# A row-form tail, and sixteen rows of one load moved to three DMA engines, in a four-layer decode attention kernel

## Chip, cores, metric

One core of one Trainium2 chip. The metric is the device time of one execution in microseconds (us), as the median of several runs; less is better.

## The reference

Four attention layers with one query token each, A, B, A, B, each with its residual. The two caches of a layer are 32 heads x 8192 positions x 192 in bfloat16; A and B have their own, and both are read twice.

```python
def _A_ref(x, k_cache, v_cache, wq, wo):          # _B_ref is the same with B's inputs
    q = (x @ wq).reshape(B, Sq, Hq, Dh) ...        # B = Sq = 1, D = 640, 32 heads of 192
    scores = einsum("bhqd,bhkd->bhqk", q, k) * (Dh ** -0.5)
    p = softmax(scores, axis=-1)
    o = einsum("bhqk,bhkd->bhqd", p, v)
    return o ... .reshape(B, Sq, Hq * Dh) @ wo
x = A_x
x = x + _A_ref(_layernorm(x), ...)                 # layer 0
x = x + _B_ref(_layernorm(x), ...)                 # layer 1
x = x + _A_ref(_layernorm(x), ...)                 # layer 2
return x + _B_ref(_layernorm(x), ...)              # layer 3
```

## The kernel before

The kernel walks 16 pairs of heads per layer. K and V of a pair are laid over 128 partitions, and `pool` is a ring of eight slots of `TS` = 12,288 columns (24,576 B in each partition) into which all loads go, in one queue issued by SyncE. `op` adds an instruction to an engine's list, with the events that it waits for; `need` issues loads up to the one asked for.

"V15" is V of a layer's last pair. In the B layers (1 and 3) its first half is one ordinary load of 128 rows of 24,576 B, and its second half comes as two quarters, the last with its own semaphore, so that the products of the last pair can start early:

```python
def transfer(n):
    ...
    if n[0] in "kv":
        h = 2 * pair(l, n[2])
        r = w[n[0]][0, h:h + 2].rearrange("h (p j) d -> (h p) (j d)", j=J)
        if quarters(n):                            # second half of V15 in layers 1 and 3
            x = TS // 2
            if n in landed:
                return SP.op(lambda s: s.dma_start(t[:, x:], r[:, TS + x:]), sem=semVQ, inc=16)
            return SP.op(lambda s: s.dma_start(t[:, 0:x], r[:, TS:TS + x]), *free, sem=semS[i], inc=16)
        if whole(*n[:3]):
            ...
        else:
            f = lambda s: s.dma_start(t, r[:, n[3] * TS:(n[3] + 1) * TS])   # V15's first half
    ...
    return SP.op(f, *free, sem=semS[i], inc=16)
```

The output projection makes y as a column, five columns of 128, with 128 columns of weights for each one-column matmul:

```python
def project(n, w, o, ev_o):
    t3 = w.rearrange("p (i n) -> p i n", n=D)
    k = t3.shape[1]
    PE.wait(ev_o, need(n), last["YB"])
    for i in range(k):
        for c in range(DC):                        # DC = 5
            e = PE.op(lambda t, i=i, c=c, ...: t.matmul(
                YB[:, c:c + 1], lhsT=t3[:, i, c:D:DC], rhs=o[:, i:i + 1], ...), ...)
    ...
```

In layer 3 the last steps are the last quarter of V15, its products, the projections of the last rows, x + y, and the result:

```python
if p == NPAIR - 1 and i == rounds // 4 and quarters(("v", nl, np_, u)):
    PE.wait(need(("vq", l)))                       # the last quarter of V15
...
if l + 1 == NL:
    return None, DV.op(lambda v: v.tensor_tensor(x_bf[:], x_true[:], YB[:, 0:DC], ALU.add), ev_y, ev_true, bank=YBu)
...
e = SP.op(lambda s: s.dma_start(out[0, 0].rearrange("(p c) -> p c", c=DC), x_bf[:]), ev_true, sem=semOUT, inc=16)
```

Of the kernel before, what the change touches and what calls it, by code (L numbers as in the profile page):

```python
# [5 lines left out]
ALU = mybir.AluOpType  # L6
# [62 lines left out]
def build(nc, A_x, A_k, A_v, A_wq, A_wo, B_x, B_k, B_v, B_wq, B_wo, out):  # L69
# [28 lines left out]
    with ExitStack() as ctx:  # L98
        def sb(name, shape, dt):
            return ctx.enter_context(nc.sbuf_tensor(name, shape, dt))  # L100
# [43 lines left out]
        vs = col(1)  # L144
        rs = col(1)
        xb = sb("xb", [P, DC], BF16)

        QM = ps("QM")
        SP_ = [ps("S0"), ps("S1")]
        OY = ps("OY", 4)  # L150
        O = OY[:, 0:VK * DH]
        YB = OY[:, VK * DH:]
        TB = ps("TB")
        use = {b: {} for b in ("QM", "S0", "S1", "O", "TB", "YB")}
        QMu, Ou, TBu, YBu = [(use[b],) for b in ("QM", "O", "TB", "YB")]
# [17 lines left out]
                                        base=0, pattern=[[-1, P]], channel_multiplier=1), e)  # L173
        PO.op(lambda g: g.memset(ones[:], 1.0))
        PO.op(lambda g: g.memset(one_b[:], 1.0))
        mask = acc[:, 0:2 * VK].rearrange("p (h i) -> p h i", h=2)
        e = PO.op(lambda g: g.memset(mask, 0.0))
        for t in range(G):
# [159 lines left out]
        def transfer(n):  # L338
            l = n[1]
            o = ORDER[l]  # L340
            w = W[l % 2]
            free = [freed[b] for b in before[n]]
            if n[0] == "wol":
                r0 = o["wol"] * PD
                return SP.op(lambda s: s.dma_start(
                    rows[:], w["wo"][r0:r0 + PD].rearrange("(p i) n -> p (i n)", p=P)),
                    *free, sem=semOL, inc=16)
            if n[0] == "t":
                return max(free, key=lambda e: e[1]) if free else None
            if n[0] == "wob":  # L350
                r0 = o["wo"][2] * PD
                return SP.op(lambda s: s.dma_start(
                    slot[place[("wo", l, 2)]][:, (NW - NB[l]) * D:NW * D],
                    w["wo"][r0:r0 + PAIRS_W * PD].rearrange("(p i) n -> p (i n)", p=P)[:, (NW - NB[l]) * D:]),
                    sem=semOB, inc=16)
            if n[0] == "vq":
                n = ("v", l, NPAIR - 1, 1)
            i = place[n]
            t = slot[i]
# [3 lines that stand above are left out]
                if quarters(n):  # L363
                    x = TS // 2
                    if n in landed:
                        return SP.op(lambda s: s.dma_start(t[:, x:], r[:, TS + x:]), sem=semVQ, inc=16)
                    return SP.op(lambda s: s.dma_start(t[:, 0:x], r[:, TS:TS + x]), *free, sem=semS[i], inc=16)
                if whole(*n[:3]):
                    if n[3] == 1:
                        return landed[n[:3] + (0,)]  # L370
                    f = lambda s: s.dma_start(pool[:, i * TS:(i + 2) * TS], r)
                else:
                    f = lambda s: s.dma_start(t, r[:, n[3] * TS:(n[3] + 1) * TS])
            elif n[0] == "wq" and l < 2:
                f = lambda s: s.dma_start(pool[:, i * TS:i * TS + DC * QW], w["wq"].rearrange("(p c) n -> p (c n)", c=DC))
            elif n[0] == "wq":
                c0, k = Q_PARTS[n[2]]
                f = lambda s: s.dma_start(
                    wq_rows(l, n[2]),
                    w["wq"][:, o["q1"] * PD:o["q1"] * PD + QC].rearrange("(p c) n -> p c n", c=DC)[:, c0:c0 + k, :])  # L380
            else:
                r0 = o["wo"][n[2]] * PD
                k = NW - NB[l] if n[2] == 2 else NW
                f = lambda s: s.dma_start(
                    t[:, 0:k * D], w["wo"][r0:r0 + PAIRS_W * PD].rearrange("(p i) n -> p (i n)", p=P)[:, 0:k * D])
            return SP.op(f, *free, sem=semS[i], inc=16)
# [53 lines left out]
        def layer(l, ev_z, ev_true):  # L440
# [82 lines left out]
            def project(n, w, o, ev_o):  # L523
# [11 lines left out]
                    freed[n] = e  # L535
                return e

            def columns(k):

                PE.wait(last["row_written"], last["TT"], ev_const)  # L540
                for i in range(k):
                    e = PE.op(lambda t, i=i: t.matmul(TB[:, i:i + 1], lhsT=orow[:, i:k * P:k], rhs=one_b[96:97, :],
                                                      start=True, stop=True), signal=(i == k - 1), bank=TBu)
                last["orow"] = freed[n] = e
                last["TT"] = AC.op(lambda a: a.activation(oT[:, 0:k], TB[:, 0:k], ACT.Copy),  # L545
                                   e, last["oT"], bank=TBu)
# [55 lines left out]
            def values(p, us=(0, 1)):  # L602
# [19 lines left out]
                for r in range(us[0] * rounds // 2, (us[-1] + 1) * rounds // 2):  # L622
                    u, i = divmod(r, rounds // 2)
                    u = turn[nl, np_][u]
                    PE.wait(need(("v", nl, np_, u)))
                    t = slot[place[("v", nl, np_, u)]]
                    if p == NPAIR - 1 and i == rounds // 4 and quarters(("v", nl, np_, u)):
                        PE.wait(need(("vq", l)))
                    for c in range(k * DH // N):
                        for g in range(G):  # L630
                            j = (i * G + g) * k
                            o, x, y = (O[32 * g:32 * g + 2 * k, c * N:(c + 1) * N],
                                       p_sb[par][:, u * JU + j:u * JU + j + k, :].rearrange("p j h -> p (j h)"),
                                       t[:, j * DH + c * N:j * DH + (c + 1) * N])
                            f, fin = r == 0, r == rounds - 1
                            e = PE.op(lambda t, c=c, g=g, o=o, x=x, y=y, f=f, fin=fin: (
                                t.matmul(o, lhsT=x, rhs=y, start=f, stop=fin) if c == 0 else  # L637
                                matmul_held(t, o, x, y, f, fin, 32, 32 * g)),
                                signal=(fin and c == k * DH // N - 1 and g == G - 1), bank=Ou)
# [43 lines left out]
            for n in [n for n in steps if n[1] == l]:  # L683
                if n[0] == "m":
                    products(*n[2:])
                elif n[0] == "s":
                    softmax(n[2])
                elif n[0] == "v":
                    values(n[2], n[3:] or (0, 1))
                elif n[0] == "e":  # L690
                    gather(n[2])
                elif n[0] == "busy":
                    busy(n[2])
                elif n[0] == "wqr":
                    q_rows(n[2], 1)
                elif n[0] == "wq":
                    q_rows(n[2], 0, 1 if l == 2 and n[2] == 0 else None)
                    q_ready = n[2] == 2 or q_ready
                elif n[0] == "wc":
                    columns(NW)  # L700
                    last["oTw"] = last["TT"]
                elif n[0] == "wo":
                    k = NW - NB[l] if n[2] == 2 else NW
                    last["oT"] = project(n, slot[place[n]][:, 0:k * D], oT[:, 0:k], last["oTw"])
                elif n[0] == "wob":
                    last["oT"] = freed[("wo", l, 2)] = project(
                        n, slot[place[("wo", l, 2)]][:, (NW - NB[l]) * D:NW * D], oT[:, NW - NB[l]:NW], last["oTw"])
                else:
                    last["TT"] = last["TTn"]
                    last["oTl"] = ev_y = project(n, rows[:], oTl, last["TTn"])  # L710
                    if l == 1:
                        busy(2)
                if q_ready and (n[0] == "wq" and l >= 2 or n[0] == "m" and n[3] == 1):
                    following = n[2] + 1 if n[0] == "m" else 1
                    if following < NPAIR and following not in ev_q:
                        q_spread(following)
                ahead()
            if l + 1 == NL:
                return None, DV.op(lambda v: v.tensor_tensor(x_bf[:], x_true[:], YB[:, 0:DC], ALU.add), ev_y, ev_true, bank=YBu)
            ev_z = DV.op(lambda v: v.tensor_tensor(z[:], xc[:], YB[:, 0:DC], ALU.add), ev_y, ev_xc, bank=YBu)  # L720
            e = DV.op(lambda v: v.tensor_tensor(x_true[:], x_true[:], YB[:, 0:DC], ALU.add), ev_y, ev_true, bank=YBu)
            last["YB"] = e
# [1 line left out]

        for l in range(NL):
            ev_z, ev_true = layer(l, ev_z, ev_true)
        e = SP.op(lambda s: s.dma_start(out[0, 0].rearrange("(p c) -> p c", c=DC), x_bf[:]), ev_true, sem=semOUT, inc=16)
        SP.wait(e)
        assert issued[0] == len(plan)

# [51 lines left out]
```

## Time and profile before

| | kernel before |
|---|---|
| median time | 1984.8 us (1984.23 to 1985.38) |
| profiled run | span 1983.6 us |
| busy: PE, DVE | 64%, 61% |
| load queue | 848.38 MB, 99.5% of the time of 16 DMA engines |
| stream, about 430 GB/s, ends at | 1978.1 us |
| last quarter of V15 landed, from there to the end | 1975.1, 8.5 us |

The kernel is bound by its loads: 848 MB at 428 GB/s. The lines that carry this stand in the prediction. One more view is used later: the stretches around the end of layer 1, in the kernel before. The columns are the stretch, its length, the busy time of PE, PEld, DVE, ACT and POOL, then the granted clock, the DMA share (1.00 is sixteen busy engines) and GB/s.

```profile
960.00:988.00 28.00, 20.72 (x83) 0.60 (x8) 25.36 (x19) 1.56 (x6) 0.00 (x0) 0.86 0.99 426
988.00:1012.00 24.00, 20.21 (x224) 5.87 (x159) 9.56 (x18) 1.89 (x7) 0.00 (x0) 0.86 0.96 395
1012.00:1040.00 28.00, 23.89 (x196) 4.91 (x94) 16.48 (x22) 3.85 (x8) 0.55 (x1) 0.87 1.00 417
```

In the middle stretch the rate dips a little, where the small last loads of the layer are.

### The profile page before, as it was taken

Reading aid. Unit: us, or ns where it says so; the run is one execution under the profiler, and the core shown is the slowest. Engines: PE = TensorE matmul, PEld = TensorE weight load, DVE = VectorE, ACT = ScalarE, POOL = GpSimd, SP = SyncE. Lnnn points to the kernel's source line nnn. Section 1 sums busy time; section 2 is a strip of 40 time slices with the busy share of each in tenths; the row PEclk is TensorE's granted clock in tenths of the full one; section 3 lists DMA queues with packets and bytes.
Section 4 is the critical chain, followed back from the end, with each engine's and each line's share of the span. In section 5 each row is a group of like instructions: output and inputs, shape, how many; then the busy total and the mean of one; then the engine's idle time right before and its main releaser. Section 6 shows DMA issues by size and latency. Waiting matters only on the chain.

```text
span 1983.6 us, 13955 instructions
## 1 busy us (share of the span) xinstructions
PE 1276.7 (64%) x8352; PEld 149.3 (8%) x3271; DVE 1200.5 (61%) x1371; ACT 139.5 (7%) x461; POOL 4.4 (0%) x22
## 2 busy tenths in 40 slices
PE   3567477666466665666785675665676765665657
PEld 0001001000100100100020010010002001001001
DVE  3566467467166656656745565665664774665665
ACT  0000000000000000000010000000000000000000
POOL 0000000000000000000000000000000000000000
PEclk9787777778687777787887777878886887778779
DMA  9999999999999999999999999999999999999998
GB/s 412 440 430 430 430 438 430 429 433 430 432 434 435 429 429 435 431 432 430 429 408 434 425 428 435 428 430 429 431 431 428 435 427 436 430 434 433 431 430 345
DMA packets 26926, 849.25 MB, mean 428 GB/s; under 512 B 3184, under 2 KB 3184, under 8 KB 3952
## 3 DMA queue, kind: packets, MB, share of 16 engines
q1 hardware_dynamic: 26720, 848.38, 99.5%
q8 instruction: 45, 0.74, 0.2%
q14 instruction: 17, 0.14, 0.0%
q10 hardware_dynamic: 144, 0.00, 0.0%
HBM read 848.36 MB, written 0.00 MB: 428 GB/s over the span
## 4 chain that ended last, share of the span: by engine, by line
DMA 67%; DVE 16%; PE 16%; ACT 1%; issue 0%; SPq 0%
DMA pool<-in_B_k_cache_dram 27%; DMA pool<-in_A_v_cache_dram 20%; DMA pool<-in_A_k_cache_dram 14%; DVE pool L560 14%; PE S L58 7%; DMA pool<-in_B_v_cache_dram 6%; PE OY L58 5%; PE OY L637 3%; DVE acc L656 1%; ACT p_sb L597 1%; DVE s_sb L582 1%; PE S L573 0%; PE OY L530 0%; DVE m_bf L584 0%; PE QM L587 0%
## 5 line engine op out<-in xcount | busy, mean ns | idle before, releaser
L560 DVE TENSOR_TENSOR pool<-pool,q_sb 128x3072 bf16<-128x3072 bf16 x512 | 861.1, 1754 | 241.0 <-DMA pool<-in_B_k_cache_dram 142.8
L58 PE MATMUL S<-pool,ident 128*128 128x512 bf16 x2944 | 784.6, 422 | 23.1 <-DVE pool L560 22.1
L667 PE MATMUL TB<-acc,small 128*1 128x192 f32 x240 | 80.6, 485 | 212.0 <-DVE acc L656 212.0
L573 PE MATMUL S<-pool,ident 128*128 128x512 bf16 x128 | 62.2, 486 | 213.9 <-DVE pool L560 213.9
L58 PE MATMUL OY<-pool,p_sb 128*16 128x512 bf16 x1920 | 199.7, 491 | 0.0
L655 DVE TENSOR_SCALAR acc<-OY,small 128x192 f32<-128x192 f32 x64 | 26.8, 418 | 278.0 <-PE OY L58 247.8
L637 PE MATMUL OY<-pool,p_sb 128*16 128x512 bf16 (+1 forms) x1216 | 147.0, 492 | 64.2 <-DMA pool<-in_A_v_cache_dram 57.8
L656 DVE SCALAR_TENSOR_TENSOR acc<-OY,small,acc 128x192 f32<-128x192 f32 x424 | 177.1, 418 | 14.9
L582 DVE TENSOR_REDUCE s_sb<-S 128x64 f32<-128x512 f32 x128 | 88.3, 690 | 68.6 <-PE S L58 68.6
L519 ACT ACTIVATE q_sb<-QM 128x192 bf16<-128x192 f32 x60 | 19.9, 331 | 954.7 <-PE QM L513 954.7
L678 ACT ACTIVATE rows<-TB,small 1x192 bf16<-1x192 f32 x120 | 43.2, 405 | 585.8 <-PE TB L667 585.8
L651 DVE RECIPROCAL small<-TB 1x2 f32<-1x2 f32 x64 | 11.2, 175 | 94.3 <-PE TB L612 75.3
L597 ACT ACTIVATE p_sb<-s_sb,small 64x128 bf16<-64x128 f32 x128 | 55.7, 435 | 162.2 <-DVE small L591 161.4
L573 PEld LDWEIGHTS S<-pool,ident 128*128 128x128 bf16 x128 | 12.9, 101 | 684.7 <-DVE pool L560 659.9
L612 PE MATMUL TB<-small,ones 128*1 128x2 f32 x120 | 11.4, 165 | 74.0 <-ACT p_sb L597 74.0
L637 PEld LDWEIGHTS OY<-pool,p_sb 128*16 128x16 bf16 (+1 forms) x1216 | 39.1, 106 | 206.2 <-issue 133.7
L587 PE MATMUL QM<-ident,m_bf 128*64 128x64 bf16 x128 | 14.0, 216 | 54.4 <-DVE m_bf L584 53.9
L667 PEld LDWEIGHTS TB<-acc,small 128*1 128x1 f32 x240 | 19.6, 100 | 311.0 <-DVE acc L656 284.7
L530 PE MATMUL OY<-oT,pool 128*128 128x1 bf16 x900 | 38.2, 178 | 2.8 <-ACT oT L545 2.8
L530 PEld LDWEIGHTS OY<-oT,pool 128*128 128x128 bf16 x900 | 37.1, 131 | 4.9 <-ACT oT L545 3.6
L591 DVE TENSOR_REDUCE small<-QM 128x1 f32<-128x64 f32 x64 | 14.4, 224 | 35.4 <-PE QM L587 35.4
L513 PEld LDWEIGHTS QM<-rows,one_b 1*64 1x64 bf16 x120 | 6.2, 100 | 349.4 <-issue 343.5
(62 smaller groups left out, 195.3 us busy)
## 6 DMA issues: line engine op xcount, KB each, us to landing
pool<-in_B_k_cache_dram SPq DMA_DIRECT2D x28, 6144.0 KB, 38.2
pool<-in_B_v_cache_dram SPq DMA_DIRECT2D x28, 6144.0 KB, 33.3
pool<-in_A_v_cache_dram SPq DMA_DIRECT2D x27, 6144.0 KB, 27.6
pool<-in_A_k_cache_dram SPq DMA_DIRECT2D x34, 3072.0 KB, 20.2
pool<-in_A_k_cache_dram SPq DMA_DIRECT2D x14, 6144.0 KB, 36.2
pool<-in_A_v_cache_dram SPq DMA_DIRECT2D x10, 3072.0 KB, 14.7
pool<-in_B_k_cache_dram SPq DMA_DIRECT2D x8, 3072.0 KB, 23.0
pool<-in_A_wo_dram SPq DMA_DIRECT2D x6, 2400.0 KB, 22.0
```

The costliest lines, as they stand in the source:

```text
L58: return t.add_instruction(mybir.InstMatmult(name=t.bass.get_next_instruction_name(), engine=mybir.EngineType.PE, ins=[t.lower_ap(rhs), t. ...
L519: lambda a: a.activation(q_sb[i][:], QM[:, 0:DH], ACT.Copy), e, last["q"][i], bank=QMu)
L530: e = PE.op(lambda t, i=i, c=c, f=y_first[0], fin=n[0] == "wol" and i == k - 1: t.matmul(YB[:, c:c + 1], lhsT=t3[:, i, c:D:DC], rhs=o[:, i ...
L560: e = DV.op(lambda v, d0=d0: v.tensor_tensor(k3[:, :, d0:d0 + QD], kin[:, :, d0:d0 + QD], q_sb[qi][:, d0:d0 + QD].unsqueeze(1).broadcast_t ...
L573: t.matmul(S[:, :], lhsT=ident[:], rhs=k3[:, :, d0:d0 + R], start=True, stop=fin) if d0 == 0 else
L582: lambda v, u=u: v.tensor_reduce(s[:, u * JU:(u + 1) * JU], SP_[u][:].rearrange("p (j r) -> p j r", r=R), AX.X, ALU.add), ev_S[p, u], last ...
L597: ev_p[p] = AC.op(lambda a, h=h, r=r: a.activation(p_sb[par][r, :, h], s[r, :], ACT.Exp, bias=negm[par][r, 0:1], accum_out=l_col[par][r, h ...
L637: t.matmul(o, lhsT=x, rhs=y, start=f, stop=fin) if c == 0 else
L655: v.tensor_scalar(acc[:], O[:, 0:DH], pick[:, 0:1], None, ALU.mult) if i == 0 else
L656: v.scalar_tensor_tensor(out=acc[:], in0=O[:, i * DH:(i + 1) * DH], scalar=pick[:, i:i + 1], in1=acc[:], op0=ALU.mult, op1=ALU.add)), e if ...
L667: e = PE.op(lambda t, h=h: t.matmul(TB[96:97, C_O + h * DH:C_O + (h + 1) * DH], lhsT=half[:, h:h + 1], rhs=acc[:], start=True, stop=True), ...
L678: last["TO"] = last["row_written"] = AC.op(lambda a, h=h: a.activation(orow[:, o0 + h * DH:o0 + (h + 1) * DH], TB[96:97, C_O + h * DH:C_O ...
```

## The change

Two ideas. The first is to take load off most DMA engines: of V15's first half, 112 rows go as one transfer, and 16 rows as five transfers of three rows and one of one row, meant for three DMA engines that the author took to be among those that end early. The prediction calls them 0, 1 and 2; these are names. The second is a shorter tail: the last projections and the result as a row (two halves of 320), x + y turned into that row beforehand, six matmuls that are only to keep the clock up before the last wait, and a result that leaves as two runs of 640 B.

```diff
+                if n[0] == "v" and n[2:] == (NPAIR - 1, 0) and l % 2:
+                    ends = [0] + list(range(112, P, 3)) + [P]
+                    for x, y in zip(ends, ends[1:]):
+                        e = SP.op(lambda s, x=x, y=y: s.dma_start(t[x:y, :], r[x:y, 0:TS]), *free, sem=semS[i], inc=16)
+                    return e
...
+            def to_row(ev):                        # after layer 3's second output projection
+                e = DV.op(lambda v: v.tensor_tensor(z[:], x_true[:], YB[:, 0:DC], ALU.add), ev, ev_true, bank=YBu)
+                ... three bfloat16 parts of z: 3 copies, 2 subtractions on DVE
+                ... 1 matmul to zero YR, 30 small ones to place the parts as a row
+            def project_row(n, w, o, ev_o):
+                ...
+                for i in range(k):
+                    for h in range(2):
+                        e = PE.op(lambda t, ...: t.matmul(
+                            YR[32 * h:32 * h + 1, :], lhsT=o[:, i:i + 1], rhs=t3[:, i, h * HD:(h + 1) * HD], ...), ...)
...
+                        if l == 3:
+                            busy(6)
                         PE.wait(need(("vq", l)))
...
-                    last["oTl"] = ev_y = project(n, rows[:], oTl, last["TTn"])
+                    last["oTl"] = ev_y = (project_row if l == 3 else project)(n, rows[:], oTl, last["TTn"])
... (likewise for layer 3's other last projections)
-                return None, DV.op(lambda v: v.tensor_tensor(x_bf[:], x_true[:], YB[:, 0:DC], ALU.add), ev_y, ev_true, bank=YBu)
+                a, m = slot[place[("wo", 3, 2)]][0:33, 0:HD], 192
+                return a, (DV.op(lambda v: v.tensor_copy(a[:, 0:m], YR[:, 0:m]), ev_y, last["oT"], bank=YBu),
+                           AC.op(lambda c: c.activation(a[:, m:], YR[:, m:], ACT.Copy), ev_y, last["oT"], bank=YBu))
...
-        e = SP.op(lambda s: s.dma_start(out[0, 0].rearrange("(p c) -> p c", c=DC), x_bf[:]), ev_true, sem=semOUT, inc=16)
+        e = SP.op(lambda s: s.dma_start(out[0, 0].rearrange("(h n) -> h n", h=2), ev_z[0:33:32, :]), *ev_true, sem=semOUT, inc=16)
```

More of the change, by code (lines that the diff above doesn't have):

```diff
@@ L146, in build @@
         xb = sb("xb", [P, DC], BF16)
+        zero = sb("zero", [P, 33], BF16)
+        part = [sb(f"part{i}", [P, DC], BF16) for i in range(3)]
         QM = ps("QM")
@@ L152, in build @@
         YB = OY[:, VK * DH:]
+        HD = D // 2
+        YR = YB[0:33, 64:64 + HD]
         TB = ps("TB")
@@ L175, in build @@
         PO.op(lambda g: g.memset(one_b[:], 1.0))
+        PO.op(lambda g: g.memset(zero[:], 0.0))
         mask = acc[:, 0:2 * VK].rearrange("p (h i) -> p h i", h=2)
@@ L536, in project @@
                 return e
+            def to_row(ev):
+                src = z
+                e = DV.op(lambda v: v.tensor_tensor(z[:], x_true[:], YB[:, 0:DC], ALU.add), ev, ev_true, bank=YBu)
+                for i in range(3):
+                    e = DV.op(lambda v, i=i: v.tensor_copy(part[i][:], z[:]), e)
+                    if i < 2:
+                        e = DV.op(lambda v, i=i: v.tensor_tensor(z[:], z[:], part[i][:], ALU.subtract), e)
+                PE.wait(e, ev_const)
+                PE.op(lambda t: t.matmul(YR, lhsT=zero[:], rhs=ident[:, 0:1].broadcast_to([P, HD]), start=True, stop=False,
+                                         skip_group_check=True), signal=False, bank=YBu)
+                for i in range(3):
+                    for c in range(DC):
+                        for h in range(2):
+                            e = PE.op(lambda t, i=i, c=c, h=h: t.matmul(
+                                YR[32 * h:32 * h + 1, c:HD:DC], lhsT=part[i][:, c:c + 1], rhs=ident[:, 64 * h:64 * h + 64],
+                                start=False, stop=False, skip_group_check=True), signal=(i == 2 and c == DC - 1 and h == 1), bank=YBu)
+            def project_row(n, w, o, ev_o):
+                t3 = w.rearrange("p (i n) -> p i n", n=D)
+                k = t3.shape[1]
+                PE.wait(ev_o, need(n))
+                for i in range(k):
+                    for h in range(2):
+                        e = PE.op(lambda t, i=i, h=h, fin=n[0] == "wol" and i == k - 1: t.matmul(
+                            YR[32 * h:32 * h + 1, :], lhsT=o[:, i:i + 1], rhs=t3[:, i, h * HD:(h + 1) * HD], start=False, stop=fin,
+                            skip_group_check=True), signal=(i == k - 1 and h == 1), bank=YBu)
+                return e
             def columns(k):
@@ L703, in layer @@
                     k = NW - NB[l] if n[2] == 2 else NW
-                    last["oT"] = project(n, slot[place[n]][:, 0:k * D], oT[:, 0:k], last["oTw"])
+                    last["oT"] = (project_row if l == 3 and n[2] == 2 else project)(n, slot[place[n]][:, 0:k * D], oT[:, 0:k], last["oTw"])
+                    if l == 3 and n[2] == 1:
+                        to_row(last["oT"])
                 elif n[0] == "wob":
-                    last["oT"] = freed[("wo", l, 2)] = project(
+                    last["oT"] = freed[("wo", l, 2)] = (project_row if l == 3 else project)(
                         n, slot[place[("wo", l, 2)]][:, (NW - NB[l]) * D:NW * D], oT[:, NW - NB[l]:NW], last["oTw"])
```

## The prediction

> **What bounds the kernel now.** I read the page first, then the stretches of the last layer, the timeline of the last 30 us, the end of the second layer, and last the completion records of the transfers.
>
> ```profile
> PE 1276.7 (64%) x8352; PEld 149.3 (8%) x3271; DVE 1200.5 (61%) x1371; ACT 139.5 (7%) x461; POOL 4.4 (0%) x22
> q1 hardware_dynamic: 26720, 848.38, 99.5%
> DMA 67%; DVE 16%; PE 16%; ACT 1%; issue 0%; SPq 0%
> ```
>
> No compute engine is over 64% busy, while the load queue fills 99.5% of the time of 16 DMA engines. 848.38 MB in 1983.6 us is 428 GB/s. The kernel streams, and nearly all of the time is the bytes.
>
> The stretches of the last layer (span, busy time of each engine, granted clock, DMA share, GB/s) say that this holds until the end:
>
> ```profile
> 1810.00:1870.00 60.00, 37.71 (x212) 2.82 (x56) 37.71 (x43) 4.06 (x14) 0.00 (x0) 0.78 1.00 432
> 1870.00:1930.00 60.00, 37.10 (x214) 2.78 (x57) 39.40 (x44) 4.06 (x14) 0.00 (x0) 0.78 1.00 434
> 1930.00:1984.00 54.00, 41.35 (x356) 8.72 (x217) 32.60 (x36) 3.46 (x13) 0.00 (x0) 0.88 0.81 346
> ```
>
> Adding up over the whole trace the time in which fewer than 16 DMA packets run gives 21 us of one engine's time (mean of 16): 8.8 before the first packet, 9 after the stream, 1.0 at the boundary of layers 1 and 2, nearly none elsewhere. Only two things can shorten the program: less for the slowest DMA engine to carry, and a shorter tail after its last byte. The change tries both.
>
> The tail in order of time:
>
> ```profile
> 1970.61 2.16 PE L530 MATMUL OY<-oT,pool 128*128 128x1 bf16 x50 [0.28 <-ACT oT L545]
> 1972.70 0.82 PE L637 MATMUL OY<-pool,p_sb 128*4 128x384 bf16 x16
> 1975.14 1.45 PE L637 MATMUL OY<-pool,p_sb 128*4 128x384 bf16 x16 [1.62 <-DMA pool<-in_B_v_cache_dram]
> ...
> 1977.57 1.04 PE L663 MATMUL TB<-small,acc 128*64 128x1 f32 x12 [0.98 <-DVE acc L656]
> 1978.54 1.16 PE L530 MATMUL OY<-oT,pool 128*128 128x1 bf16 x25
> 1979.56 0.74 PE L530 MATMUL OY<-oTl,rows 128*128 128x1 bf16 x15
> 1980.34 0.16 DVE L719 TENSOR_TENSOR x_bf<-small,OY 128x5 bf16<-128x5 f32 x1 [2.82 <-PE OY L530]
> 1980.53 0.35 SPq L727 DMA_DIRECT2D out_dram<-x_bf  x1
> ```
>
> The last quarter of V15 landed at 1975.10 and PE had waited 1.62 us for it. The same 16 matmuls took 0.82 us before that wait and 1.45 after: the clock fell. Two stretches around it show 1.00 and 0.50 in the clock column:
>
> ```profile
> 1961.00:1974.00 13.00, 10.75 (x151) 4.70 (x124) 3.91 (x11) 1.89 (x7) 0.00 (x0) 1.00 0.94 393
> 1975.00:1981.00 6.00, 4.18 (x68) 3.01 (x68) 1.00 (x3) 0.27 (x1) 0.00 (x0) 0.50 0.08 31
> ```
>
> A transfer ends with 16 increments of its semaphore, and their times spread. For the last quarter of V15 in layer 3 the first came 5.62 us before the last (1969.47 and 1975.10); six came more than 4.3 us early. In layer 1 the spread was 6.14 us, with six more than 5.2 early. So some DMA engines run dry while the slowest still has 5 us to do. The trace does not say which number each engine has.
>
> [...]The trace agrees that 128 rows give 16 completions; no transfer in it uses fewer. [...]the result leaves now as 128 runs of 10 B, and its completions come 1.33 to 2.71 us after issue.
> [...]The trace agrees: 1.00 before 1974.68, 0.50 after.
> [...]the kernel's helper orders such users by semaphore, so I expect the two final copies one after the other. No run yet shows it.
>
> **The change, part by part.**
>
> (a) V15's first half. A row is 24,576 B; such a packet has a median of 0.913 us in the trace. Before: 8 rows an engine. After: 7 on engines 3 to 15, 12 on engines 1 and 2 (7+5), 13 on engine 0 (7+5+1). Relief of 13 engines: 0.91 us in each of layers 1 and 3, 1.83 in all. Extra: 3.65 us a layer on engines 1 and 2, 4.56 on engine 0. If those three are among the early ones, layer 1 is safe: 5.2 to 6.1 early against 4.6. In layer 3 it is tighter. At the boundary after layer 1 the spread shrank from 6.14 to 2.23 because early engines stood idle some 3.5 us; engine 0 will not stand idle there. It starts layers 2 and 3 some 1 to 2 us later relative to the rest, and takes 4.56 more at the end. Over both layers it has 9.1 us more and gets back 3.5 of idling and 5.5 of earliness: it ends within a fraction of a microsecond of the old slowest. So the gain at the last landing lies between 0 and 1.83; I take 1.2 to 1.3.
> Six more issues of 0.33 to 0.43 us cost SP some 2.5 us, but the next issue of that queue waits 16 us anyway (1920.96 to 1936.87 in layer 3), and the ring holds tens of microseconds of work (27 to 43 us from issue to landing). Nothing.
>
> (b) Turning x + y into the row, after the second output projection of layer 3. Six 128x5 DVE operations at 0.16 us and 31 small matmuls, estimated 1.2 and 2 us. Where they fall:
>
> ```profile
> 1801.84 3.16 PE L530 MATMUL OY<-oT,pool 128*128 128x1 bf16 x75 [0.28 <-ACT oT L545]
> 1809.57 13.44 DVE L560 TENSOR_TENSOR pool<-pool,q_sb 128x3072 bf16<-128x3072 bf16 x8 [10.75 <-DMA pool<-in_B_k_cache_dram]
> ```
>
> DVE is idle 10.75 us, 4.5 of it after the projection ends at 1805.0, and PE's next work comes at 1811.4. Hidden: 0.
>
> (c) The last products. 50, 25 and 15 one-column matmuls with 128 columns of weights become 20, 10 and 6 of 320 columns with one column of weights, two column groups side by side. 320 columns at the rate of the 128x512 group (12 of 512 columns in four groups in about 0.64 us, so 0.21 for 512) are 0.13 us a pair. The first goes from 2.16 to about 1.5 us, ahead of the landing. The other two go from 1.73 (end of the 12 fp32 matmuls at 1978.61 to DVE's start at 1980.34) to about 1.35 at full clock, but to about 2.3 at half clock.
>
> (d) Six filler matmuls before the wait for the last quarter: 6 x 0.22 = 1.3 us. PE got to that wait at 1973.5; with 0.6 saved in (c) it gets there near 1972.9 and leaves the filler at 1974.2. That lies inside the old wait, but it limits how much of an earlier landing is used: start max(1974.2, 1975.1 minus the gain of layer 3), both less the gain of layer 1. In return the 16 matmuls should run at 0.82, not 1.45 (-0.6), and the fp32 group some 0.2 faster. The clock's windows may still drop it during the last products, so on the mean of both cases I put (c)'s end at -0.1.
>
> (e) The end. A DVE copy of 33x192 from PSUM (from 0.16 for 5 columns and 0.69 for 512: about 0.35 us), then an ACT copy of 128 columns (from 0.19 for 15 and 0.33 for 192: about 0.28), one after the other: 0.7 with the hop, against 0.16 before: +0.5. The result leaves as 2 runs of 640 B in place of 128 of 10 B: I expect about 1.7 us where the last completion took 2.71: -1.0.
>
> Sum: start of the last V15 products -1.3, those products -0.6, fp32 group -0.2, projections -0.1, copies +0.5, result transfer -1.0: -2.7 us. 1984.8 - 2.7 = 1982.1.
>
> **Rivals.** Engine 0 becomes the last: if it is not an early one, it ends later than the slowest did, layer 1 is delayed too, and (a) costs up to 3 us or more. Against it: three early engines are needed of six, and the authors picked them; the spread repeats transfer after transfer. Time then about 1984 to 1986.
> The filler or the clock eats the gain: the filler ends after the landing, and the clock drops anyhow; the row form at half clock costs 0.6. Then about 1983.5.
> All goes well: engine 0 is 5.5 early in both layers, the clock holds through the projections and the two copies overlap: -4.0, about 1980.8.
> A hidden cost of (b), a K slot freed late, is spoken against by the 4.5 us of slack and the full ring.
>
> **Range and chances.** The best case gives 1980.8, the worst likely one about 1984.5. The terms are each under 2 us and 2% is 40 us, beyond anything that the change touches: only a new stall of the stream could do it. 8 in 10: 1980.3 to 1984.3.
>
> **What would show it.** The three stretches of the last layer stay at 430 GB/s or above; the boundary of layers 1 and 2 comes up to 0.9 us earlier; the last quarter's wait disappears behind the filler or shrinks below 0.5 us; the 16 matmuls after it take 0.8; the projections about 0.7 and 0.4; two copies in sequence; the result in under 2 us. Wrong, if engine 0's completion of V15's first half is the last of the 16 by more than 1 us, if DVE's wait of 10.75 us before that K grows, or if the result transfer still takes 2.7 us.

"1.00 before 1974.68, 0.50 after" is the granted clock, and "such users" are the users of one PSUM bank, `YBu` in the kernel.

## The result, and the profile after

The changed kernel takes **2013.1 us** (2011.3 to 2015.25, 4 runs; the profiled one 2009.5) against 1984.8 in the same rounds. The ratio is 1.0143, 95% interval 1.0128 to 1.0159. (A ratio here and below is the mean time of one kernel's fast runs over that of the other's fast runs of the same rounds, so not quite the ratio of the medians.) Executions over 1.5% slower than the fastest of the same kernel are left out of the means. It is 1.4% slower, 28 us where -2.7 was forecast, and far above the range.

The page of the kernel after, in the lines that answer to those shown of before (engines, load queue, chain), with its GB/s in 40 slices of the span:

```profile
PE 1286.9 (64%) x8335; PEld 149.0 (7%) x3249; DVE 1201.3 (60%) x1377; ACT 139.6 (7%) x462; POOL 4.5 (0%) x23
...
GB/s 415 430 435 428 435 433 429 435 432 427 434 435 429 434 429 433 433 433 431 358 365 430 427 430 435 427 431 434 427 430 428 435 435 429 435 429 433 433 431 235
...
q1 hardware_dynamic: 26612, 848.38, 99.6%
...
DMA 65%; PE 19%; DVE 14%; ACT 1%; another core or an unknown queue 1%; issue 0%; SPq 0%
```

The same slices of the kernel before:

```profile
GB/s 412 440 430 430 430 438 430 429 433 430 432 434 435 429 429 435 431 432 430 429 408 434 425 428 435 428 430 429 431 431 428 435 427 436 430 434 433 431 430 345
```

This is the most instructive pair of lines. PE and DVE work about as long as before (64% and 60% for 64% and 61%), the load queue moves the same bytes, and its share is still 99.6%: the sixteen DMA engines count as busy all the time. Only the bytes per second tell: two slices in the middle (358 and 365 for 429 and 408) and the last (235 for 345), the ends of layers 1 and 3. A high busy share of DMA says that packets are in flight, not that they move at full rate.

The stretches around the end of layer 1 and the end of layer 3, after:

```profile
960.00:988.00 28.00, 21.29 (x82) 0.60 (x8) 25.09 (x18) 2.01 (x7) 0.00 (x0) 0.81 0.99 426
988.00:1012.00 24.00, 12.14 (x96) 1.14 (x29) 8.82 (x16) 1.70 (x6) 0.00 (x0) 0.85 1.02 212
1012.00:1040.00 28.00, 22.23 (x239) 8.88 (x200) 10.36 (x18) 0.87 (x3) 0.55 (x1) 0.76 0.95 375
```
```profile
1890.00:1960.00 70.00, 45.78 (x253) 2.98 (x62) 48.02 (x53) 5.37 (x19) 0.00 (x0) 0.79 1.01 434
1963.00:1990.00 27.00, 16.15 (x114) 1.28 (x30) 12.10 (x18) 1.70 (x6) 0.00 (x0) 0.82 1.00 235
```

From 988 to 1012 the DMA share is 1.02 and the rate 212, where before it was 395: half. In layer 3 the same from 1963 to 1990.

The trace's packet records say which packets (a packet here is one row of a transfer, moved by one engine). They are summed here over each layer's end; the time is the sum over all packets of that size, divided by 16 engines:

| layer 3, from 1930 us to the end of the stream | before: mean us, total | after: mean us, total | difference |
|---|---|---|---|
| 24,576 B, V15's first half (128) | 0.916, 7.33 | 1.919, 15.35 | +8.0 |
| 12,800 B, a `wo` load just before it (128) | 0.483, 3.87 | 0.762, 6.10 | +2.2 |
| 12,288 B, the two quarters after it (256) | 0.464, 7.42 | 0.675, 10.80 | +3.4 |
| sum | | | **+13.6** |

In layer 1 the same sum is 13.2. The last landing of layer 1 moved from 1012.59 to 1026.24 us (+13.65), and the end of the stream from 1978.14 to 2005.46 (+27.3, twice that). So all but about half a microsecond of the later end (13.6 + 13.2 of 27.3) lies in these two places, and four tenths of it (2.2 + 3.4 of 13.6) are in packets that the change did not touch.

PE's wait in the end of layer 3, after:

```profile
PE OY L679 <- DMA pool<-in_B_v_cache_dram: 14.7, 1, 14.7
```

The tail after it, in order of time (start, busy us, engine, line, operation; in brackets the idle time before it and what ended it):

```profile
1995.31 2.73 PE L679 MATMUL OY<-pool,p_sb 128*4 128x384 bf16 x32 [14.67 <-DMA pool<-in_B_v_cache_dram]
...
2001.66 1.24 PE L58 MATMUL S<-ident 128*128 128x512 bf16 x5
...
2002.83 0.82 PE L679 MATMUL OY<-pool,p_sb 128*4 128x384 bf16 x16
...
2004.63 0.89 PE L705 MATMUL TB<-small,acc 128*64 128x1 f32 x12 [0.98 <-DVE acc L698]
2005.45 0.84 PE L573 MATMUL OY<-pool,oT 128*1 128x320 bf16 x10
2006.13 0.57 PE L573 MATMUL OY<-rows,oTl 128*1 128x320 bf16 x6
2006.74 0.35 DVE L764 CAST pool<-OY 33x192 bf16<-33x192 f32 x1 [2.17 <-PE OY L573]
2007.13 0.27 ACT L765 ACTIVATE pool<-OY 33x128 bf16<-33x128 f32 x1 [1.30 <-DVE pool L764]
2007.47 0.60 SPq L773 DMA_DIRECT2D out_dram<-pool  x1
```

The wait of 14.67 us for V15's first half is new; before, there was none at this place. The rest is the shorter tail as planned: 0.82 for the 16 matmuls after the last quarter (landed at 2002.39), and 7.1 us from that landing to the end where it was 8.5. That is the forecast -1.4, as a sum: the filler made the 16 matmuls start 0.4 us after the landing, and the projections gained 0.4 more than forecast, which cancel. So the tail did what it should, and the loss is in the split.

### The profile page after: what moved, and what is told of

Same layout as the page of the kernel before. It is cut to its first block, busy times and chain, and to the rows that moved or that the text cites. A ratio compares the mean times of both kernels' runs of the same rounds, so it can differ in the third digit from the quotient of the medians.

```text
span 2009.5 us, 13938 instructions
## 1 busy us (share of the span) xinstructions
PE 1286.9 (64%) x8335; PEld 149.0 (7%) x3249; DVE 1201.3 (60%) x1377; ACT 139.6 (7%) x462; POOL 4.5 (0%) x23
## 3 DMA queue, kind: packets, MB, share of 16 engines
q1 hardware_dynamic: 26612, 848.38, 99.6%
## 4 chain that ended last, share of the span: by engine, by line
DMA 65%; PE 19%; DVE 14%; ACT 1%; another core or an unknown queue 1%; issue 0%; SPq 0%
DMA pool<-in_B_k_cache_dram 26%; DMA pool<-in_A_v_cache_dram 20%; DMA pool<-in_A_k_cache_dram 14%; DVE pool L600 12%; PE S L58 9%; PE OY L58 5%; DMA pool<-in_B_v_cache_dram 4%; PE OY L679 3%; DVE acc L698 1%; ACT p_sb L637 1%; DVE s_sb L622 1%; PE S L613 1%; PE OY L540 0%; DVE m_bf L624 0%
```

## The experiments

The theory on seeing this was that the partitions that a transfer writes set its rate, so that one of 112 rows runs at half the rate (1.92 us a packet for 0.916). The expectations call it "ports". That is a name here: what in the hardware would do it no run shows. The rivals: the three-engine transfers or their number of issues stall the queue, or the row form does harm where it looks hidden.

**row_only** and **split_only**: each half of the change alone. row_only removes the five added lines in `transfer`; split_only is the kernel before with those lines.

> The changed kernel with the split of V15's first half undone (one transfer of 128 rows again), row form, filler and row result kept. Both theories, 'the 112-row transfer[...]' (ports) and 'the small transfers on three engines hold everything up' (three engines), expect the whole loss gone and the tail's gain left: in the two traces the last quarter's landing to the end took 8.5 us before and 7.1 after, so 1984.8 - 1.4 = 1983.4, with V15's first half landing at about 1002 and 1968 as before. A theory that the row form costs the 28 us expects about 2013.

Measured: 1982.75 us (1982.6 to 1983.61, before 1984.59), ratio 0.999 [0.9978, 1.0003].

> The kernel before with nothing but the split of V15's first half (112 rows, then five transfers of 3 rows and one of 1). Ports and three engines: all of the loss, 2013 + 1.4 = about 2014.5, with packets of 24,576 B at 1.8 us or more in both places. If the row form were the cause: about 1985.

Measured: 2012.06 us (2010.3 to 2015.64), ratio 1.0139 [1.0125, 1.0153]. The whole loss is the split's. Whether the two parts add up to a microsecond is not shown: the runs of split_only scatter over 5 us, and the changed kernel, which should be 1.8 us under it, has a median 1.0 above it. The 24,576 B packets took 1.84 us on the mean in layer 1, and 1.76 in layer 3, a little under the 1.8 expected. The row form gained 1.8 us in the medians and 2.7 in the profiled spans (1980.9 against 1983.6); the interval of the ratio still touches 1. The turning of x + y into a row, in row_only:

```profile
1805.92 0.16 DVE L546 TENSOR_TENSOR small<-small,OY 128x5 f32<-128x5 f32 x1 [6.84 <-PE OY L535]
...
1807.15 0.45 PE L552 MATMUL OY<-ident,zero 128*33 128x320 bf16 x1 [1.27 <-DVE part L548]
...
1807.53 1.76 PE L557 MATMUL OY<-ident,part 128*1 128x64 bf16 x30
1809.81 5.10 DVE L595 TENSOR_TENSOR pool<-pool,q_sb 128x3072 bf16<-128x3072 bf16 x3 [2.72 <-DMA pool<-in_B_k_cache_dram]
```

DVE still waits 2.72 us for the next K after the last of the six operations, and PE has ended at 1809.3, before its next work: hidden.

**one_of_16**: is it the transfers of three rows? The 16 rows go as one transfer.

```diff
-                    ends = [0] + list(range(112, P, 3)) + [P]
+                    ends = [0, 112, P]
```

> The changed kernel, but the 16 rows go as one transfer of 16 rows[...]; the 112-row transfer stays. Ports: the 112 rows still run at half rate (7 rows x 1.88 us = 13.2 us instead of 7.3 for 8 rows)[...] so +6 to +9.5 us a layer, 1995 to 2002 us, with 24,576 B packets at 1.8 us or more. Three engines: no loss, 1983 to 1985, packets at 0.91.

Measured: 2011.47 us (2009.19 to 2014.58), ratio 1.0135 [1.0121, 1.0149]; 24,576 B packets 1.86 us on the mean in layer 3. Without any three-row transfer the loss is nearly the same: neither the three engines nor the number of issues is needed for it. The size was missed: 1995 to 2002 was expected. (Of its +6 to +9.5 us a layer, 13.2 - 7.3 = 5.9 are from measured packets.)

Two numbers show what the three engines may have added in layer 3. The last of the 16 completions of V15's last quarter came 1.95 us after the one before it in the changed kernel and 1.57 in split_only, but 0.35 in one_of_16. One engine did trail; which one, the trace does not say.

**by_columns**: keep all 128 partitions in the large transfer and still unload the 13 engines. All 128 rows bring seven eighths of their columns as one transfer; the rest comes by three engines (123 rows in one transfer) and five rows. (Its profile page counts 26,852 packets in the load queue, 136 a layer more than from_7's 26,580 with one transfer of 128 rows: 128 for the added rows, and 8 completions, as three and five engines give.)

```diff
-                    ends = [0] + list(range(112, P, 3)) + [P]
-                    for x, y in zip(ends, ends[1:]):
-                        ... s.dma_start(t[x:y, :], r[x:y, 0:TS]) ...
+                    c = TS - TS // 8
+                    for x, y, i0, i1 in ((0, P, 0, c), (0, 123, c, TS), (123, P, c, TS)):
+                        ... s.dma_start(t[x:y, i0:i1], r[x:y, i0:i1]) ...
```

> The changed kernel with the same relief cut another way: the first seven eighths of the columns for all 128 rows by 16 engines, the last eighth of 123 rows by three engines (41 rows of 3,072 B each, 126 KB, 4.7 us at 26.9 GB/s) and 5 rows by five.[...] Ports: no slowdown of packets beyond the few that meet the three engines' writes; between row_only's time and 1.8 us less, 1981.6 to 1983.8. Three engines (they are overloaded or hold the others up): slower than row_only by 4 us or more.

Measured: 1992.9 us (1992.34 to 1993.58), ratio 1.0041 [1.0027, 1.0055], against 1984.6. It lost 8 us. The theory called "ports" missed (it expected 1981.6 to 1983.8), and the rival's expectation, slower than row_only by 4 us or more, came true with 10. The 21,504 B packets of the 128-row transfer ran at full rate (0.80 us, which is 0.913 x 7/8) as long as they were alone; those that began after 1965.8, once the 3,072 B packets of the three engines ran beside them (from 1965.1), took 1.12 to 1.46, and the 3,072 B packets 0.20 where 0.114 would be the full rate. So the transfer on three engines does harm here, and slows packets of a transfer of 128 rows. How it does so, no trace shows.

**from_7** and **to_7**: is it the side read or the side written? from_7 writes all 128 partitions and was to read the source in steps of seven rows; to_7 writes 112 partitions and reads in steps of eight. Both give wrong values.

```diff
+                    f7 = bass.AP(r.tensor, r.offset, [[7 * 2 * TS, 16], [2 * TS, 8], [1, TS]])
+                    return SP.op(lambda s: s.dma_start(t, f7), *free, sem=semS[i], inc=16)
```
```diff
+                    f8 = bass.AP(r.tensor, r.offset, [[8 * 2 * TS, 16], [2 * TS, 7], [1, TS]])
+                    SP.op(lambda s: s.dma_start(t[0:112, :], f8), *free, sem=semS[i], inc=16)
+                    return SP.op(lambda s: s.dma_start(t[112:P, :], r[112:P, 0:TS]), *free, sem=semS[i], inc=16)
```

> row_only with the rows of V15's first half read from a wrong place (wrong result on purpose)[...]. Ports (the writing side is what matters): as row_only, 1982 to 1984, packets of 24,576 B at 0.91 us. A rival, the reading side[...]: the loss of the changed kernel, 1997 to 2012, packets at 1.8.

Measured: 2010.04 us (2008.22 to 2014.1), ratio 1.0134 [1.0118, 1.0149]; packets 1.81 and 1.86 us in the median of layers 3 and 1. The theory called "ports" was missed as written.

> one_of_16 with the source steps put back (wrong result on purpose): 112 partitions written, 7 an engine[...]. Ports: all of one_of_16's loss, about 2011, packets at 1.8. Reading side: 1983 to 1986, packets at 0.91 except the 16-row transfer.

Measured: 2012.56 us (2011.37 to 2013.02), ratio 1.0138 [1.0122, 1.0153]; packets 1.79 and 1.83 us in the median of layers 3 and 1. So the loss of a 112-row transfer does not need the reading in steps of seven rows.

from_7 can be reconciled with the theory if a source of 16 groups of eight also changes which partitions each engine writes. That needed its own test.

**same_by_8** was to be that test: the right rows, with the source written as 16 groups of eight.

> row_only with the same rows from the same addresses to the same partitions in one transfer, only written as 16 groups of 8 rows on the reading side[...] (right result). from_7 had changed this grouping too, so it did not tell the reading from the writing side. Ports[...]: as slow as from_7, about 2010, packets at 1.8. Rival, the reading side: what was slow in from_7 was reading at 7-row steps, so this one is as fast as row_only, 1983. If the grouping is merged away by the compiler: also 1983, and the issue takes 0.33 us as in row_only, not 0.66.

Measured: 1982.95 us (1982.61 to 1983.41), ratio 0.9991 [0.9975, 1.0007]. Its one issue took 0.328 us in layer 1 where from_7's took 0.66, and the trace gives the destination as one dimension of 128: the groups had been merged into a plain transfer. Nothing follows but a repeat of row_only, and the explanation of from_7 stays untested.

**halves** and **middle**: does it matter which 64 partitions are written? halves brings rows 0 to 63, then 64 to 127; middle brings rows 32 to 95 first, then the outer rows in thirds of the columns, so that their packets are told apart by size.

```diff
+                    ends = [0, 64, P]                                    # halves
```
```diff
+                    c = TS // 3                                          # middle
+                    for x, y, i0, i1 in [(32, 96, 0, TS)] + [(x, x + 32, i0, i0 + c) for x in (0, 96) for i0 in range(0, TS, c)]:
+                        ... s.dma_start(t[x:y, i0:i1], r[x:y, i0:i1]) ...
```

> row_only with V15's first half sent as two transfers of 64 rows, 4 rows an engine (right result, no odd count, all 16 engines). Ports:[...] packets near 1.8 us, 14.6 us instead of 7.3 a layer, so 1997, or up to 2010 if the transfers around it are caught as in the changed kernel. If it were the odd 7 or the three engines: 1982 to 1985.

Measured: 2013.01 us (2009.42 to 2014.42), ratio 1.0139 [1.0125, 1.0153]; packets 1.85 us in the median; the first three took 1.2 to 1.4, and 125 of the 128 over 1.5.

> row_only with V15's first half cut into partitions 32 to 95 first (64 rows, 4 an engine, packets of 24,576 B) and then 0 to 31 and 96 to 127 in thirds of the columns (2 rows an engine, packets of 8,192 B; at full rate 0.305 us). Ports:[...] as long as the middle runs its packets take 0.91 to 1.0 us, where the first 64 in halves took 1.8; the outer ones[...] 0.6 us a packet. In time: the loss is smaller than in halves, some 1995 to 2005. Rival, any cut into transfers of 64 rows or less is slow, whichever the rows: 24,576 B packets at 1.8 from the first on, 2010.

Measured: 2001.8 us (1998.68 to 2003.17), ratio 1.0083 [1.0067, 1.0099]. The 24,576 B packets took 0.91 to 0.92 while they were alone, and all 34 that began after 1966, once the outer rows ran, 1.66 or more. The outer 8,192 B packets took 0.59 (0.305 at full rate, a third of 0.914). Two transfers of 64 rows, the same size, and the one to partitions 32 to 95 is twice as fast (0.91) as the one to 0 to 63 or 64 to 127 (1.85). The stretches of middle show it as a rate:

```profile
1961.00:1965.00 4.00, 3.63 (x16) 0.00 (x0) 4.00 (x4) 0.00 (x0) 0.00 (x0) 1.00 0.98 418
1966.00:1972.00 6.00, 6.00 (x68) 0.70 (x21) 3.34 (x9) 0.98 (x4) 0.00 (x0) 1.00 1.02 228
```

**write_middle** and **read_middle** settle the side ("Theory 1" in the expectations is the side written). As middle, but for the 24,576 B packets one side alone is moved: write_middle writes partitions 32 to 95 and reads rows 0 to 63; read_middle reads rows 32 to 95 and writes partitions 0 to 63. The other partitions follow in thirds, read from their own rows (in read_middle as transfers of 64 rows). Their outputs are wrong, which doesn't matter for the times.

```diff
+  for x, q, m, i0, i1 in [(32, 0, 64, 0, TS)] + [(x, x, 32, i0, i0 + c) for x in (0, 96) for i0 in range(0, TS, c)]:   # write_middle
+  for x, q, m, i0, i1 in [(0, 32, 64, 0, TS)] + [(64, 64, 64, i0, i0 + c) for i0 in range(0, TS, c)]:                  # read_middle
+                        ... s.dma_start(t[x:x + m, i0:i1], r[q:q + m, i0:i1]) ...
```

> Wrong on purpose: as the run with the middle rows first, but the 24,576 B packets are read from rows 0 to 63 of V15 and written to partitions 32 to 95; then partitions 0 to 31 and 96 to 127 in thirds of the columns, read from their own rows. Theory 1[...]: the 24,576 B packets take 0.91 us while they run alone, and 1.7 us once the thirds run, and the time is about 2002 as in that run. Theory 2 (the side read, rows 0 to 63): the 24,576 B packets take 1.8 us from their first on, and the time is 2005 or more.

Measured: 1999.63 us (1998.34 to 2001.31), ratio 1.0077 [1.0061, 1.0093].

> Wrong on purpose, the mirror image: the 24,576 B packets are read from rows 32 to 95 of V15 and written to partitions 0 to 63; then partitions 64 to 127 in thirds of the columns, read from their own rows. Theory 1[...]: the 24,576 B packets take 1.8 us from their first on, as with the two halves, and the time is about 2012 or more. Theory 2 (the side read): they take 0.91 us while they run alone, and the time is about 2002.

Measured: 2012.36 us (2010.42 to 2014.86), ratio 1.0141 [1.0125, 1.0157]. The packet records of layer 3:

| 24,576 B packets | first began | lowest us | first over 1.3 us at | over 1.5 us |
|---|---|---|---|---|
| write_middle | 1961.1 | 0.91 | 1965.0 (the thirds begin at 1964.8) | 34 of 64 |
| read_middle | 1965.7 | 1.32 | 1965.7, its first | 62 of 64 |

The stretches, first of write_middle, then of read_middle (its first stretch holds only earlier loads):

```profile
1961.00:1965.00 4.00, 4.00 (x20) 0.00 (x0) 3.65 (x3) 0.00 (x0) 0.00 (x0) 1.00 1.01 419
1966.00:1972.00 6.00, 6.00 (x68) 0.59 (x15) 3.84 (x10) 0.98 (x4) 0.00 (x0) 1.00 0.94 206
```
```profile
1961.00:1965.00 4.00, 4.00 (x18) 0.10 (x1) 4.00 (x3) 0.00 (x0) 0.00 (x0) 0.90 0.93 395
1966.00:1972.00 6.00, 5.57 (x51) 0.37 (x14) 4.42 (x5) 0.00 (x0) 0.00 (x0) 1.00 0.97 207
```

Where write_middle's large packets run alone the rate is 419; read_middle's bring it to 207 from their start. Both came out as the theory of the side written had said, and against the side read: for these transfers of 64 rows, which partitions are written sets the rate, and which rows are read does not.

**no_filler**: row_only without the six matmuls before the last wait.

```diff
-                        if l == 3:
-                            busy(6)
```

> row_only without the six filler matmuls before the wait for V15's last quarter. If the filler holds the clock up as intended: the 16 matmuls after the wait take 1.4 us instead of 0.82 and the projections run at half clock (1.3 and 0.8 us a group instead of 0.84 and 0.57), +1.0 to +1.5 us, 1984.0. If the denser row form alone keeps the clock: no change, 1982.7.

Measured: 1983.63 us (1983.25 to 1985.32, before 1984.67), ratio 0.9996 [0.9983, 1.001]. Its tail, then the same matmuls of row_only:

```profile
1974.70 0.82 PE L672 MATMUL OY<-pool,p_sb 128*4 128x384 bf16 x16 [2.31 <-DMA pool<-in_B_v_cache_dram]
...
1976.50 1.04 PE L698 MATMUL TB<-small,acc 128*64 128x1 f32 x12 [0.98 <-DVE acc L691]
1977.47 1.49 PE L568 MATMUL OY<-pool,oT 128*1 128x320 bf16 x10
...
1978.76 1.00 PE L568 MATMUL OY<-rows,oTl 128*1 128x320 bf16 x6
```
```profile
1974.25 0.82 PE L674 MATMUL OY<-pool,p_sb 128*4 128x384 bf16 x16 [0.67 <-DMA pool<-in_B_v_cache_dram]
...
1976.04 0.90 PE L700 MATMUL TB<-small,acc 128*64 128x1 f32 x12 [0.98 <-DVE acc L693]
1976.87 0.84 PE L568 MATMUL OY<-pool,oT 128*1 128x320 bf16 x10
...
1977.55 0.57 PE L568 MATMUL OY<-rows,oTl 128*1 128x320 bf16 x6
```

Without the filler the clock falls at 1975.94: too late for the 16 matmuls (0.82 in both), but the projections run at half clock, 1.49 and 1.00 in place of 0.84 and 0.57. From the landing of the last quarter to the last completion of the result it is 7.5 us (1974.65 to 1982.15) in place of 6.3 (1974.20 to 1980.49): the filler is worth 1.2 us in the profile, 0.9 in the medians (the intervals of the two ratios overlap).

**one_copy**: row_only with DVE copying all 320 columns.

```diff
-                return a, (DV.op(lambda v: v.tensor_copy(a[:, 0:m], YR[:, 0:m]), ev_y, last["oT"], bank=YBu),
-                           AC.op(lambda c: c.activation(a[:, m:], YR[:, m:], ACT.Copy), ev_y, last["oT"], bank=YBu))
+                return a, (DV.op(lambda v: v.tensor_copy(a[:, 0:HD], YR[:, 0:HD]), ev_y, last["oT"], bank=YBu),)
```

> row_only with the result copied out of PSUM by DVE alone, 320 columns at once, instead of 192 by DVE and then 128 by ACT. The two ran one after the other (0.35 + 0.04 + 0.27 = 0.66 us in the changed kernel). One copy: 0.16 + 320 x 1.04 ns = 0.49 us, so -0.17 us, within the noise of the runs, visible in the timeline: 1982.6.

(The 1.04 ns a column are from the prediction's two DVE instructions: 0.69 us for 512 columns and 0.16 for 5.)

Measured: 1982.45 us (1982.38 to 1984.68), ratio 0.9992 [0.9979, 1.0005].

```profile
1979.23 0.48 DVE L759 CAST pool<-OY 33x320 bf16<-33x320 f32 x1 [2.17 <-PE OY L568]
```

One copy takes 0.48 us; the two in sequence took 0.35 + 0.27 and a gap of 0.04. Those 0.2 us cannot be seen in the times. It has the lowest median of all the kernels run, some 30 us under the changed kernel, but its gain over the kernel before lies inside the interval.

## Why the prediction was wrong

**The step that failed is (a)**, in its first sentences: "A row is 24,576 B; such a packet has a median of 0.913 us in the trace. Before: 8 rows an engine. After: 7 on engines 3 to 15". The size of a packet was taken to set its time, whichever partitions its transfer writes. It measured 1.92 us on the mean, 15.35 us of each engine's time for V15's first half in place of 7.33, and a further 5.6 us in the packets beside it. 13.6 us in layer 3 and 13.2 in layer 1 are nearly all of the 27.3 us by which the stream ends later. The rival "engine 0 becomes the last", at up to 3 us, had the wrong mechanism for the loss as well as the wrong size: the mean over sixteen engines accounts for it. It may be a small part: one engine trails by 1.95 us in layer 3, against 0.35 in one_of_16. The numbers of engines held: V15's first half has 32 completions in layer 3, which is 16 + 5 x 3 + 1, and its last four packets there are three side by side (from 1989.32, 1989.74 and 1989.75) and one after them (1992.14 to 1994.26), as 12, 12 and 13 rows on three engines would end.

What the runs show of the cause: the time is the split's (split_only); it does not need the three-engine transfers (one_of_16); in transfers of 64 rows the partitions written set the rate, and not the rows read (write_middle, read_middle); partitions 32 to 95 run at 0.91 while alone, and 0 to 63 and 64 to 127 at 1.85 (middle, halves). Some things stay open. Why the one range of partitions is fast and the others are slow, no run shows. For the 112 rows themselves the side written is argued from the transfers of 64: no run wrote 112 partitions at full rate. Which seven rows each engine takes of 112 is not in the trace. Why from_7, which wrote all 128 partitions, was as slow (1.81) is not shown. And the slowing of fast packets once others run beside them is measured, in by_columns (0.80 to between 1.12 and 1.46) and middle (0.91 to 1.66 or more), but how it comes about is not.

Would a version that keeps all 128 partitions in the large transfer have had the gain of 0 to 1.83 us? by_columns, the one that was run, did not: it lost 8 us, and the packets beside those of the three engines slowed. No other such split was run.

The range failed because of "only a new stall of the stream could do it": the case was named, and then given no weight. Changing 128 partitions into 112 in the stream that bounds the kernel was the one edit able to make such a stall.

**(b) held**: nothing lost, 2.72 us of DVE's wait left in row_only. **The issues held**: seven in 2.3 us, with no engine running dry.

**(c)** was put at -0.1 on the mean of two clocks, 1.35 or 2.3 for 1.73. That is a slip: their even mean is 1.83, which is +0.1. Measured from the end of the fp32 group, 1.22 at full clock (1976.94 to 1978.16 in row_only), and 2.27 at half clock in no_filler (1977.54 to 1979.81). So both cases were nearly right, and with the filler the better one holds, -0.5.

**(d) held**: 0.82 for 1.45 and 0.90 for 1.04. But in no_filler's profile its use lies elsewhere than forecast: the 16 matmuls ran at 0.82 without it, and the gain is in the projections. That is partly chance. The clock fell at 1975.94 there, after the 16 matmuls, and at 1974.68 in the kernel before, ahead of them. The filler also ended at 2002.8 in the kernel after, 0.4 after the landing: that limit was forecast.

**(e) held**: two copies in sequence, 0.35 + 0.04 + 0.27, and the result in 1.60 us from issue to last completion where it took 2.71.

Of the clock the trace of the kernel before shows the halving (1.00 and 0.50 are its only values) and fixed windows: all of its 206 stretches of one clock but the last are whole multiples of 3.41 us long (changes at 1831.32, 1834.74 and 1844.98, one and three times 3.41 us apart). When the clock fell at 1974.68, PE had been idle since 1973.52, 1.16 us.

One reading in the prediction goes too far, without weight in its sum: of the 21 us of missing DMA time the packet records of the kernel before show 12.3 inside the span: 2.0 in its first 20 us, not 8.8, and 8.8 at its end.

Terms (b) to (e) without the earlier landing sum to -1.4 in the prediction; the tail took 7.1 us for 8.5 in the kernel after, and 6.7 in row_only. Where the split is undone the time is 1982.75, by chance near the 1982.1 forecast, which counted on 1.3 us from the split that did not come.

## What to carry to other kernels

In a kernel bound by its loads, leave the full transfers over 128 partitions whole; to take 16 rows out of one of them cut the rate of the stream around it from 395 to 212 GB/s here (end of layer 1). Judge a stream by its bytes per second and the time of one packet, not by the busy share of its engines, which stayed at 99.6% here. And when a forecast counts on small terms, ask which single edit could touch the bound itself, and give that case its weight.
